# A new order of the operations of a fused attention and feed-forward kernel

## The chip, the cores and the metric

The kernel runs on one core of a Trainium2 chip. The core has engines that run their own instruction queues in order and wait for each other through semaphores: TensorE (PE, with the weight loads shown apart as PEld), VectorE (DVE), ScalarE (ACT), GpSimd (POOL) and SyncE (SP, which only issues DMAs here). The metric is the device time of one execution in microseconds. Before the change the median of three runs is 359.96 us (360.23, 359.96 and 359.49).

## The reference

Attention with a squared ReLU in place of a softmax, and a feed-forward layer with an exact GELU behind it:

```python
q, k, v: (8, 12, 448, 64)           # batches, heads, rows, head width
scores = q @ k^T / sqrt(64)
attn   = max(scores, 0) ** 2 / 448
x      = (attn @ v), heads side by side   # 3584 x 768
h      = x @ w_in                    # 768 x 2048
g      = 0.5 * h * (1 + erf(h / sqrt(2)))
out    = g @ w_out                   # 2048 x 768, float32
```

There is no sum over a row of scores, so the tiles of scores are independent of each other.

## The kernel before

**Loads and turning.** GpSimd loads Q, K, V and the weights with DMAs that cast float32 to bf16 (`nk`, `nq`, `v_sb`, `win_sb`, `wout_sb`). Scores need K and Q with the head width on the partitions (`kT`, `qT`). For batches 0 and 1 TensorE turns them (L620 and L648, tile `tp`) and VectorE or ScalarE copies the result out (L519, L521). For batches 2 to 7 SP issues DMA transposes (L675), one for K and one for Q of each head group; a head group is four heads, a batch has three. Some loads of later batches stand on GpSimd behind a small copy (L709, L717, tile `gate`) that waits until a Q transpose has landed, since the loads write over what the transposes read.

**Attention.** For each batch, head group and block of 128 keys (two heads of 64): scores (L752, `ps`), ReLU with scale into bf16 (L769 on ScalarE or L771 on VectorE, `a_sq`), the square (L781 on VectorE or L779 on ScalarE). When all seven blocks of a head group are done comes the product with V, called AV here (L831, `pav`), whose result is copied to `xT` (L519 or L521). In batches 0 and 1 some scores and AVs are done in halves of 224 rows.

**First product of the feed-forward layer.** A part of batch 0 is done plainly (L891, `psh`, GELU L901). Most of it is done in units by a scheme of seven products in place of eight (L1048, `pe`; sums of x `t_x` L1007, sums of weights `ws` L962), whose partial results VectorE and ScalarE add up (L1086, L519, L521, `part`) before GELU (L1098) writes `h_sb`. The last batch has its own form (L1199, L1236, L1245, L1164).

**Second product.** It goes by groups of 256 output rows (L1375, `pso`, with sums of hidden rows `s_sb` L1356 and sums of weights `t_sb` L1309). Passes add up the products into an output tile `osb` (L1409, L519 and L521); there are three output tiles. Each half of a group, 128 rows, is stored by SP when its passes are done (L1328, L1336). In the first batches a store of 128 rows is issued in two pieces, since attention rows lie in DRAM in four strides of 112.

**What sets the order.** Every step is an object `Op` with the engines that may do it, what it depends on and which buffers it takes and frees: three score tiles of two PSUM banks each (`w`), two more PSUM banks (`f`), 14 tiles `a_sq`, three output tiles. A string `ORDER` (lines 84 to 171, 1618 words) lists all of them. The letter of a word is the engine: P for TensorE, Q for TensorE with the two halves of a score tile in two separate banks of `f`, A ScalarE, D VectorE, G GpSimd, S the DMAs of SP. The number is the step, by the order in which the code creates it. Z is a product of zeros with so many columns (`fill`, L1677) that writes nothing that is used. `place()` walks through the string and puts each step at the end of its engine's queue, so the queue of each engine is the string's words of that engine in the string's order; nothing is decided at run time. Before the string's first words stand the loads of the first part of K and Q and nine products of zeros (`spin`, L1510).

Of the kernel before, what the change touches and what calls it, by code (L numbers as in the profile page):

```python
# [83 lines left out]
G0 G1616 G1 G3 G4 G7 D13 Z1024 A10 G118 A16 G2 P14 D15 P11 D12 P17 D18 P19 D20 P42 A43 P36 A37 P33  # L84
P21 D44 D22 P23 A24 D34 P51 P25 A52 D26 P48 Q39 D35 G117 P54 A49 D40 P63 A64 D55 P57 P27 D28 P29 D30
P69 P66 A58 D59 P31 D32 A70 D71 A67 G121 G6 G125 D38 P90 P93 D41 A94 D65 P131 A132 P102 A103 P129
P45 A46 A47 G126 Z672 A91 P84 D130 Q159 D50 D68 P72 G5 A160 D85 G8 G122 A73 G120 P111 A112 A53 D56
D74 P75 P133 D76 P156 D113 A157 A134 P81 D82 P139 A140 P60 D61 D83 P96 P108 D62 A97 D109 P137 P78
A79 D86 D80 P174 A175 D77 D92 P135 A136 D95 G124 P171 A172 D104 D98 P87 A88 P105 D89 A106 P168 A169
P141 A142 P162 D107 D110 D138 P195 A163 P99 D100 Q114 G119 P207 D101 D176 P165 A196 A115 D116 A158  # L90
P198 A199 D173 P143 A144 D208 D170 A166 D197 P240 A241 A161 D250 D251 P180 D181 D167 G128 G123 G9
D164 P222 A223 P192 P242 A243 P244 D253 D209 P145 A193 A146 P213 A214 A245 D194 P177 A178 D200 P189
A179 P183 D215 D190 D191 P246 A184 A247 P210 D182 A211 P216 P186 A187 D185 P248 A249 P258 P275 A217
D254 G127 G236 D188 P219 A276 G235 G238 G147 A220 Q201 D224 D212 D255 G148 P204 A202 A203 A205 D252
A221 P260 P277 A206 D259 P261 P278 A262 D409 D280 D218 D257 P265 D256 P282 A283 A266 Q225 A279 D412
D263 P270 P267 A226 A227 D371 D372 P284 D268 A269 P287 D285 P375 A264 A281 P392 A393 P273 G150 D271
P290 D288 P382 P399 D447 D374 A376 P378 P395 A274 D373 D450 A289 A291 D448 G151 P377 D451 P394 D397
A286 A400 A383 P387 P404 D380 A396 A379 P384 A272 D405 A406 P401 D388 P413 P430 A389 A414 A431 D385
A386 P420 P437 A421 D402 S228 A438 P407 D452 P390 D410 P416 A391 D411 P433 A408 D455 P442 S229 D454
A417 A434 P415 A398 G153 G154 P432 D443 A444 D435 A436 D418 P422 P439 A403 Q299 A300 P314 A315 P425  # L100
D423 P428 D456 D426 P459 A427 A424 D440 G234 A419 P311 P317 P445 P461 A441 D453 D449 D457 A318 D460
S230 S231 P463 P323 D312 A429 A381 A446 A313 D462 S232 P308 D316 S233 D301 A324 D309 D464 P350 P465
D466 A351 D352 P305 P302 A306 D310 P335 A307 P467 G237 G149 G152 G155 D458 D336 D468 A303 D304 P469
D470 P326 A327 P365 A366 P341 A342 D319 P471 P338 G239 G292 A339 A340 P320 D491 D472 A321 P332 A322
D337 D492 D343 G293 G294 D493 A333 P329 G295 D330 D367 S475 S476 P495 G296 A496 P497 P353 D498 P359
D334 D360 A331 A354 P362 A363 P499 S473 A500 P501 P356 P347 D325 A364 D328 P344 A357 A358 D355 D348
G297 D361 D345 D346 D349 G481 P511 A512 P520 A521 P503 P517 D502 A518 P526 P368 A369 D527 A519 P514
D504 S477 S478 G484 D494 S479 S480 P529 P505 D370 D583 P587 A513 P604 P507 D584 D515 G298 P594 A530
G487 A588 P589 A595 D605 D586 D522 A528 P607 P590 D508 D585 D592 P611 A516 P606 D608 A591 G482 G483
D621 D609 P599 A612 G485 G486 P596 S657 D531 P613 G488 D600 A601 S658 G489 S510 P623 P640 G663 D597  # L110
D614 P616 D617 A610 A641 A624 D622 P602 D506 P619 P625 P642 A593 A615 A603 A620 A598 Q523 D628 D645
A524 A646 P535 P626 P643 D525 S509 A536 A627 P630 P647 P538 A539 D631 D644 Q532 D533 A618 A534 P571
A572 P632 D648 P649 D673 P635 Q550 P553 A554 P652 D650 A651 D633 P638 P655 A656 D551 D674 A639 D636
A637 P677 P577 D653 A654 P559 A560 P547 S659 P679 D552 D675 P565 D548 S660 A678 D680 A578 A555 D540
P562 D563 D537 A566 S661 A567 D676 P681 P683 A682 D684 A634 P541 P574 P544 A545 D546 A629 A564 G666
P685 D686 S474 D542 D543 D693 D694 G490 P687 D688 S691 P689 D690 P568 A575 A549 A569 P556 D695 P719
A557 A558 A720 P713 D714 P697 D698 P725 A726 A727 A576 P728 D729 P722 D696 A570 P699 S692 D700 P731
P737 D732 P701 D702 D723 P703 P705 P746 D579 S662 G669 G664 G665 A561 D573 A747 P580 G667 A581 D704
D706 D730 D582 D785 P716 P709 A717 D710 S712 G668 G670 D786 P789 D788 G671 P806 A724 D790 P791 D794
D807 A738 P796 P813 D814 P707 A718 D787 A733 D715 P808 A739 D811 D708 A721 A812 P809 P792 D823 A810  # L120
P749 A750 Q734 D793 P740 A741 A795 D797 P798 P815 D816 P818 D819 D799 A742 A735 A736 D748 P825 P842
A843 P801 P821 P804 A751 A805 Q770 D802 P752 S711 A822 D826 P828 P845 A846 P832 D824 D753 D829 P849
D875 P827 S859 S860 S861 P844 D754 A850 P854 A800 S862 P834 P851 A771 A803 P879 D855 D830 D852 A833
D835 D847 P837 A817 A820 A853 P840 P857 P764 D876 D838 P755 D765 D877 A880 P883 A756 D878 A836 A858
A831 P773 A774 P761 D762 P881 D882 A841 G865 G868 A848 A884 P743 A763 A839 P767 D768 P918 D766 A775
P885 D886 P887 G672 D757 D888 A744 A856 A919 D745 P889 D890 D772 S893 P933 A934 D895 A935 P758 A759
D896 P779 A780 P776 A777 S863 A760 P891 P899 A900 S864 D898 P945 P927 D892 A778 P921 A922 A928 D946
D781 A947 P903 D920 P901 D897 P942 P948 A949 D769 D943 P782 A783 P924 G871 D902 A904 P930 D929 D931
D932 A925 P905 D906 A784 P907 D908 G866 P951 P915 D923 P939 D987 P909 G867 A940 D926 G869 G870 G872
D910 D988 P911 D912 S914 A952 P991 P1008 A916 A917 D990 Q963 D964 D944 P957 G873 A953 S1061 A958  # L130
D959 P936 A937 Q954 A938 P998 P1015 D992 P993 P1010 D1009 S1062 D989 A999 D950 P1011 A1016 A955
D1013 A1014 A956 P994 D996 P1003 D1012 A995 P1020 P1027 D1025 P1044 P1000 D1021 A1022 D1004 D1028
A1045 D1001 P1029 A997 P1046 D1049 A1050 D1032 A1005 P1030 P1047 D1026 P1017 D1018 A1031 P1034 P1051
D1048 S1063 S1064 S1065 A1002 P1023 P1036 P1053 D1052 D1054 A1035 D1037 P1039 P1056 P1006 G1067
A1007 G1070 D1057 D1079 A1024 P1042 P1059 A1060 P1081 D1040 S913 P978 A1041 A1043 A1058 P1117 D941
A979 P960 A961 D1077 D1078 D1118 P1150 D1151 S894 D962 P1120 P1083 A1121 P966 P972 A1082 P969 A973
P1085 P1141 D980 D967 D1084 A970 D1086 A968 D974 D1080 P981 A982 G874 A1055 P975 P1087 D1088 D1142
P1089 A1033 D1090 A976 P1091 A983 A1019 D1092 A1038 P1144 P1132 D1097 D977 P1147 A965 D971 A1133
A1148 D1134 P1093 P1101 D1094 S1095 S1066 P1129 A1130 P984 A1119 P1126 D1099 D1098 P1103 A985 A986
D1102 P1105 D1104 D1127 A1106 A1145 P1107 P1135 A1131 P1123 P1156 A1124 D1122 P1109 D1143 P1195  # L140
G1073 G1068 A1125 D1136 A1157 P1193 D1189 P1212 G1069 G1071 G1072 D1137 A1149 S1263 P1210 D1108
D1110 P1111 D1100 P1113 G1074 D1128 A1211 D1215 P1165 A1194 G1075 D1198 D1112 S1115 A1199 A1166
A1167 D1114 P1138 D1190 D1192 S1264 S1265 Q1153 S1096 P1200 P1217 P1196 P1213 A1139 A1154 D1140
A1218 Q1177 A1201 D1227 A1197 P1159 A1160 P1205 A1214 P1222 D1191 A1216 P1229 P1246 P1219 D1223
A1224 S1116 D1206 D1178 A1247 D1220 P1231 S1266 P1248 D1251 S1267 A1230 G1617 P1232 P1249 A1161
A1221 P1202 A1233 D1234 A1235 P1225 A1250 D1228 A1207 D1158 D1203 A1226 P1236 P1253 A1152 P1238
# [1568 lines left out]
```

## Time and profile before

| | |
|---|---|
| median of three runs | 359.96 us |
| the profiled execution | 360.24 us |
| its span | 358.5 us |
| TensorE busy | 350.0 us, 98% |
| VectorE busy | 305.6 us, 85% |
| ScalarE busy | 270.3 us, 75% |
| GpSimd busy | 102.9 us, 29% |
| mean granted clock of TensorE | 0.999 |

The span is the time from the first to the last recorded instruction or transfer; the execution takes 1.74 us more. A row of the timeline gives the start in us from the start of the span, the length, the engine, the line, the operation, the tiles (written <- read) and the shapes; in brackets stands how long the engine had been idle and what released it. SPq and POOLq rows are the issue of a DMA, not its transfer. A row of the DMA issues gives the time from issue to landing at its end. A row of the groups gives busy time, mean length in ns, idle time ahead and its releasers.

### The profile page before, as it was taken

The page shows a single profiled execution, that of the slowest core. Times are in us where ns is not written, and L with a number is a line of the kernel's source. Part 1 is how long each engine was busy: PE and PEld are TensorE (multiplying, and loading weights), DVE is VectorE, ACT ScalarE, POOL GpSimd, SP SyncE. Part 2 cuts the span into 40 slices and gives each one's busy share as a digit, 9 for nine tenths or more (in the row PEclk, how much of TensorE's full clock was granted, in tenths as well). Part 3 has the DMA queues.
Part 4 walks back from the last instruction along what each step waited for, and adds up shares of the span by engine and source line. Part 5 has one row for each costly group of instructions (what it writes and reads, how often), then busy time and mean ns, then how long its engine had stood idle before and what let it go on. Part 6 is the DMA issues. An engine that isn't in the chain of part 4 may idle for free.

```text
span 358.5 us, 9223 instructions
## 1 busy us (share of the span) xinstructions
PE 350.0 (98%) x3841; PEld 248.0 (69%) x3841; DVE 305.6 (85%) x515; ACT 270.3 (75%) x437; POOL 102.9 (29%) x138
## 2 busy tenths in 40 slices
PE   8879999999999999999999999999999999999995
PEld 3557679955588655896557965579668855788663
DVE  2999999999997989988889898779988998595762
ACT  3999997899869896978978669789986778334300
POOL 8664816096193104700075100841000000000000
PEclk9999999999999999999999999999999999999999
DMA  9999999999999958995399941998402001012222
GB/s 171 197 201 204 201 204 157 146 145 148 183 141 146 214 84 127 154 169 79 63 90 159 214 69 51 88 171 209 72 3 90 2 0 46 3 44 90 88 87 91
DMA packets 124361, 43.01 MB, mean 120 GB/s; under 512 B 102688, under 2 KB 120992, under 8 KB 124320
## 3 DMA queue, kind: packets, MB, share of 16 engines
q0 software_dynamic: 85328, 22.47, 66.2%
q1 hardware_dynamic: 38448, 19.50, 26.0%
q8 instruction: 30, 0.49, 0.5%
q10 hardware_dynamic: 544, 0.46, 0.4%
q14 instruction: 11, 0.09, 0.1%
HBM read 45.61 MB, written 11.01 MB: 158 GB/s over the span
## 4 chain that ended last, share of the span: by engine, by line
PE 92%; ACT 5%; DVE 2%; issue 0%; DVEq 0%; ACTq 0%
PE pso L1375 37%; PE pe L1048 30%; PE ps L752 9%; PE pav L831 8%; PE pb L1199 4%; ACT a_sq L769 3%; PE psh L891 2%; PE spin L1510 1%; DVE a_sq L781 1%; DVE a_sq L771 1%; ACT xT L521 0%; PE tp L620 0%; PE fill L1677 0%; ACT a_sq L779 0%; ACT qT L521 0%
## 5 line engine op out<-in xcount | busy, mean ns | idle before, releaser
L769 ACT ACTIVATE a_sq<-ps 128x896 bf16<-128x896 f32 (+1 forms) x125 | 106.7, 893 | 14.5 <-PE ps L752 14.2
L781 DVE TENSOR_TENSOR a_sq<-a_sq 128x896 bf16<-128x896 bf16 (+1 forms) x108 | 63.8, 615 | 2.1 <-ACT a_sq L769 1.9
L1375 PEld LDWEIGHTS <-s_sb 128*128 128x128 bf16 x456 | 42.4, 98 | 32.3 <-issue 7.1
L1048 PEld LDWEIGHTS <-win_sb 128*128 128x128 bf16 x624 | 59.5, 98 | 2.7 <-issue 1.5
L771 DVE TENSOR_SCALAR a_sq<-ps 128x896 bf16<-128x896 f32 (+1 forms) x57 | 55.5, 988 | 2.6 <-PE ps L752 2.2
L779 ACT ACTIVATE a_sq<-a_sq 128x896 bf16<-128x896 bf16 x61 | 57.2, 959 | 0.5
L752 PE MATMUL ps<-qT,kT 64*64 64x448 bf16 (+1 forms) x756 | 49.7, 337 | 2.7 <-ACT a_sq L769 1.3
L1098 ACT ACTIVATE h_sb<-part 128x448 bf16<-128x448 f32 x78 | 43.2, 580 | 9.9 <-DVE part L1086 9.7
L1086 DVE TENSOR_TENSOR part<-pe,part 128x448 f32<-128x448 f32 x78 | 45.5, 620 | 5.3 <-PE pe L1048 3.6
L1375 PEld LDWEIGHTS <-h_sb 128*128 128x128 bf16 x336 | 31.9, 98 | 22.9 <-issue 4.0
L1048 PEld LDWEIGHTS <-ws 128*128 128x128 bf16 x468 | 44.1, 98 | 3.5 <-issue 2.9
L1375 PE MATMUL pso<-wout_sb,s_sb 128*128 128x384 bf16 (+2 forms) x232 | 41.1, 321 | 0.0
L1375 PE MATMUL pso<-t_sb,s_sb 128*128 128x384 bf16 x224 | 41.1, 327 | 0.0
L1375 PE MATMUL pso<-wout_sb,h_sb 128*128 128x384 bf16 x224 | 41.1, 327 | 0.0
L559 POOL DMA_DIRECT2D nk<-in_k_dram x36 | 34.7, 968 | 9.6 <-DMA wout_sb<-in_moe_w_out_dram 8.1
L831 PE MATMUL pav<-a_sq,v_sb 64*64 64x448 bf16 (+1 forms) x756 | 36.5, 329 | 0.8 <-DVE a_sq L781 0.8
L752 PEld LDWEIGHTS <-kT 64*64 64x64 bf16 x756 | 19.6, 105 | 23.7 <-issue 17.7
L1048 PE MATMUL pe<-t_x,win_sb 128*128 128x224 bf16 x312 | 34.5, 259 | 0.0
L1048 PE MATMUL pe<-xT,win_sb 128*128 128x224 bf16 x312 | 34.1, 259 | 0.0
L1048 PE MATMUL pe<-t_x,ws 128*128 128x224 bf16 x312 | 33.2, 259 | 0.0
L521 ACT COPY part<-pe 128x448 f32<-128x448 f32 x53 | 26.4, 541 | 8.9 <-PE pe L1048 6.2
L1409 DVE TENSOR_TENSOR osb<-pso,p_sb 128x384 f32<-128x384 f32 x42 | 23.3, 554 | 9.4 <-PE pso L1375 5.9
(74 smaller groups left out, 409.5 us busy)
## 6 DMA issues: line engine op xcount, KB each, us to landing
out_dram<-osb SPq DMA_DIRECT2D x19, 384.0 KB, 2.8
nq<-in_q_dram POOLq DMA_DIRECT2D x38, 112.0 KB, 5.8
nk<-in_k_dram POOLq DMA_DIRECT2D x36, 112.0 KB, 5.8
v_sb<-in_v_dram POOLq DMA_DIRECT2D x5, 672.0 KB, 7.6
v_sb<-in_v_dram POOLq DMA_DIRECT2D x9, 224.0 KB, 8.0
win_sb<-in_moe_w_in_dram POOLq DMA_DIRECT2D x8, 192.0 KB, 9.2
wout_sb<-in_moe_w_out_dram POOLq DMA_DIRECT2D x4, 384.0 KB, 12.7
wout_sb<-in_moe_w_out_dram POOLq DMA_DIRECT2D x1, 1536.0 KB, 15.8
```

Source lines behind the costliest of these rows:

```text
L521: A.copy(dst, src)
L559: nc.gpsimd.dma_start(nk[b][:, g0, :, e], rows[:, e].rearrange("p (i d) -> p i d", d=D))
L752: nc.tensor.matmul(side(ps, e)[64 * j : 64 * j + 64, x * w : x * w + w], kT[r, g, i * 128 + 64 * j : i * 128 + 64 * j + 64], moving, start ...
L769: A.activation(to, x, AF.Relu, scale=c_att)
L771: V.tensor_scalar(to, x, c_att, 0.0, op0=mybir.AluOpType.mult, op1=mybir.AluOpType.max,)
L779: A.activation(ar, ar, AF.Square)
L781: V.tensor_mul(ar, ar, ar)
L831: nc.tensor.matmul(side(pav[0], e)[o2 : o2 + 64, :w], vt[b][r, 2 * g + e, bass.ts(i, D)], box["a2"][r, e, o : o + w], start=(i == 0), stop ...
L1048: nc.tensor.matmul(bank[name][:, y, z * HS : z * HS + HS], w[:, k, bass.ts(mm, 128)], right()[:, k], start=first and k == 0 and z == 0, st ...
L1086: V.tensor_add(get(to), ps(name), get(other))
L1098: A.activation(h_ring()[:, m : m + 2, o + half[c].start : o + half[c].stop], src().rearrange("p (x n) -> p x n", x=2), AF.Gelu,)
L1375: nc.tensor.matmul(box[bank][:, n0:n1], left()[:, kf], right()[:, kf, n0:n1], start=bool(need) and kf == 0, stop=kf == K2 - 1, skip_group_ ...
```

## The change

The string `ORDER` is replaced; nothing else changes. The same 1618 steps are listed. 101 steps move from ScalarE to VectorE and 91 the other way: among them, ScalarE has 121 of the full-width ReLUs where it had 116, 59 of the squares where it had 61, 21 of the AV copies where it had 33. The queue of GpSimd is unchanged. On TensorE most steps shift by a few places; six score or AV steps change between the two kinds of banks. On SP some stores and transposes change places. The lines with the beginning and with the first stores:

```diff
@@ -84,88 +84,88 @@
-G0 G1616 G1 G3 G4 G7 D13 Z1024 A10 G118 A16 G2 P14 D15 P11 D12 P17 D18 P19 D20 P42 A43 P36 A37 P33
+G0 G1616 G1 G3 G4 G7 D13 Z1024 A10 G118 A16 Z672 P14 D15 G2 P11 D12 P17 P33 D34 G117 A18 P36 A37 P21
...
-D337 D492 D343 G293 G294 D493 A333 P329 G295 D330 D367 S475 S476 P495 G296 A496 P497 P353 D498 P359
+P356 P499 A357 G297 D333 D325 A334 D355 P501 P347 A364 S474 D358 A348 S473 S475 S476 A500 P359 D360
...
```

On TensorE at the start of the program (`fill` are the products of zeros, `tp` the first turning of K), before:

```order
L1510 MATMUL spin_106<-zero_100 128x512
L1677 LDWEIGHTS zero_100
L1677 MATMUL fill_130<-zero_100 64x512
L1677 LDWEIGHTS zero_100
L1677 MATMUL fill_130<-zero_100 64x512
L620 LDWEIGHTS nk_119
L620 MATMUL tp_140<-ident_95,nk_119 64x128
```

and after:

```order
L1677 MATMUL fill_130<-zero_100 64x512
L1677 LDWEIGHTS zero_100
L1677 MATMUL fill_139<-zero_100 64x512
L1677 LDWEIGHTS zero_100
L1677 MATMUL fill_139<-zero_100 64x160
L620 LDWEIGHTS nk_119
L620 MATMUL tp_142<-ident_95,nk_119 64x128
```

The second product of zeros, of 672 columns, has moved from the 28th place among TensorE's steps to the one behind the first.

On SP near 85 us, before: the transposes of batch 2's last head group (`kT_1483`, `qT_1482`), those of batch 3's first (`kT_1856`, `qT_1855`), and the store of rows 128 to 255 in two pieces. The store of rows 0 to 127 stands 14 places further behind.

```order
L675 DMA_TRANSPOSE kT_1483<-nk_1148 128x7x128
L675 DMA_TRANSPOSE qT_1482<-nq_1147 128x8x112
L675 DMA_TRANSPOSE kT_1856<-nk_1148 128x7x128
L675 DMA_TRANSPOSE qT_1855<-nq_1147 128x8x112
L1336 DMA out_0_dram<-osb_1697 96x768
L1336 DMA out_0_dram<-osb_1697 32x768
```

and after, with batch 2 as `kT_1212` and `qT_1211`, batch 3 as `kT_1936` and `qT_1935`, and both stores:

```order
L675 DMA_TRANSPOSE kT_1212<-nk_904 128x7x128
L675 DMA_TRANSPOSE qT_1211<-nq_903 128x8x112
L1336 DMA out_0_dram<-osb_1683 112x768
L1336 DMA out_0_dram<-osb_1683 16x768
L1336 DMA out_0_dram<-osb_1742 96x768
L1336 DMA out_0_dram<-osb_1742 32x768
L675 DMA_TRANSPOSE kT_1936<-nk_904 128x7x128
L675 DMA_TRANSPOSE qT_1935<-nq_903 128x8x112
```

Four store pieces now stand ahead of the first K and Q transposes of batch 3. The first of them waits for the last pass of rows 0 to 127. On VectorE, before, that pass is the third row from the end here:

```order
L1409 TENSOR_TENSOR osb<-pso,osb 128x384
L781 TENSOR_TENSOR a_sq<-a_sq 128x896
L1409 TENSOR_TENSOR osb<-pso,p_sb 128x384
L781 TENSOR_TENSOR a_sq<-a_sq 128x896
L1356 TENSOR_TENSOR s_sb<-h_sb 128x1024
L1409 TENSOR_TENSOR osb<-pso,osb 128x384
L781 TENSOR_TENSOR a_sq<-a_sq 128x896
L1356 TENSOR_TENSOR s_sb<-s_sb,h_sb 128x1024
```

and after it is the last row:

```order
L1409 TENSOR_TENSOR osb<-pso,osb 128x384
L781 TENSOR_TENSOR a_sq<-a_sq 128x896 x2
L1409 TENSOR_TENSOR osb<-pso,p_sb 128x384
L1356 TENSOR_TENSOR s_sb<-h_sb 128x1024
L1356 TENSOR_TENSOR s_sb<-s_sb,h_sb 128x1024
L1356 TENSOR_TENSOR s_sb<-h_sb 128x1024
L1409 TENSOR_TENSOR osb<-pso,osb 128x384
```

The pass has moved behind all three sums of hidden rows.

More of the change, by code (lines that the diff above doesn't have):

```diff
@@ L89 @@
[L89 to L103, printed above, removed]
@@ L109 @@
[L109 to L123, printed above, removed]
@@ L124 @@
[L124 to L134, printed above, removed]
@@ new lines @@
+D134 D82 D140 A80 A112 D98 P156 P135 D92 P141 D83 D136 P168 G128 A157 G123 G9 A77 G127 G236 D104
+P174 A142 A169 P87 D113 D88 D89 D110 Q171 A172 P162 P99 A163 D175 D176 G235 G238 Q114 A100 A101 P195
+D161 P213 G147 A115 G148 G150 G151 G153 D164 A116 D252 P165 A166 A196 D214 D167 P143 A144 P240 P192
+P180 A241 A193 P222 D197 A223 A181 P244 A245 P242 D158 P198 A199 D173 D250 P207 A243 D170 D182 D208
+P177 A178 P189 A179 D190 D191 P183 A184 P145 A146 P204 A185 D251 P186 P210 P248 A187 A205 D200 D254
@@ new lines @@
+P246 D255 D188 A249 A247 A211 P258 P275 P219 A220 D194 D209 A259 D253 D224 Q201 A276 P216 A217 A218
+D257 P260 S228 S229 D215 P261 P278 D202 A279 P277 P265 P282 A262 D256 G154 P267 P284 D263 A206 A283
+P287 A264 D221 D212 A203 D409 Q225 A226 A227 D285 S230 A286 D266 P270 D280 G234 D268 P273 A274 D288
+D371 P375 P392 A393 A281 A376 P290 D271 D372 D374 P382 P399 A269 A291 P395 A383 A400 P378 P377 P394
+P387 A396 A379 A289 D447 D373 P384 D412 P401 D410 D397 A398 D380 P413 D388 A389 P404 D385 P430 A386
@@ new lines @@
+P905 A784 D906 D929 A947 P939 A940 P915 P942 D943 A926 P907 D908 P909 D941 D987 D988 D910 P911 D912
+A916 D917 P991 A920 P1008 D990 Q963 D964 P957 A923 P936 Q954 A958 A953 P998 P1015 A950 A1016 D989
+D937 D938 P993 D992 P1010 D1009 D1013 D996 P994 D955 P1011 A999 P1003 A995 P1020 G869 A1012 G870
+G872 D1021 A1022 D1004 P1027 P1044 S914 D1025 P1000 D1001 P1029 P1046 D1026 A997 A1028 D1032 S1061
+A1045 D1049 A959 G873 P1030 P1017 A1014 P1047 D1048 P1006 A1002 P1034 A1033 P1051 A944 A1005 D1031
+P1036 P1053 D1018 P1023 D1035 D965 A1052 P1056 D1037 S1062 D1054 P1039 A1024 S893 D1077 A1055 A1007
@@ new lines @@
+P1042 A1043 Q1117 S913 A1118 D956 P960 D1040 D1057 P966 A1041 D967 D1078 A1038 A961 A962 P1059 A1060
+P1081 P1120 A1082 S1063 S1064 D968 A1121 P978 D1079 P972 D979 D980 A973 D974 P1083 P975 A976 P1123
+P969 A970 A1050 P1085 D1124 P1135 A1019 P1141 P981 A1058 A1142 D1084 D1086 P1087 A1119 D982 A983
+D1080 P1089 G1067 D1088 A1136 P1091 D977 P1132 P1147 A1148 D971 D1097 P984 D1090 G1070 D1133 A1134
+P1150 G874 D1151 A985 D986 D1092 S1095 P1144 A1145 P1093 D1094 D1143 P1126 A1127 A1128 S1065 D1098
@@ new lines @@
+P1156 P1129 A1130 D1100 D1131 P1101 P1195 P1212 S1066 G1073 G1068 D1102 G1069 D1125 P1193 P1210
+D1099 A1211 D1215 A1216 P1103 D1104 P1105 P1107 D1194 D1198 A1157 D1106 D1108 P1109 D1110 D1191
+P1111 D1112 D1189 P1113 D1114 D1190 A1137 P1165 A1158 A1122 P1138 D1139 A1199 A1166 Q1153 A1154
+P1200 P1217 D1192 A1146 A1201 D1140 P1196 D1155 P1213 D1227 G1071 P1159 G1072 A1218 A1214 Q1177
+S1263 A1160 P1222 A1178 D1197 P1205 D1206 P1229 P1246 A1247 D1223 A1224 P1219 D1220 P1231 P1248
+D1179 A1230 A1149 D1234 P1202 D1203 P1232 A1207 P1249 A1235 G1074 A1221 A1233 D1251 A1252 D1250
@@ new lines @@
+S1116 S1264 P1208 A1209 D1228 P1236 G1075 P1253 S1265 S1266 P1238 A1237 D1239 G1617 A1254 D1167
+P1225 P1241 D1242 A1204 P1255 D1256 A1226 A1240 A1161 P1171 Q1168 D1169 A1243 A1172 S1096 P1258
+D1152 D1259 P1244 P1261 A1257 Q1174 P1162 A1262 A1245 S1267 A1260 D1175 A1176 D1269 D1270 P1183
+A1184 D1185 P1301 A1302 P1273 D1271 D1274 P1275 P1307 D1272 A1308 P1180 D1276 A1163 P1277 A1181
+A1170 D1164 P1279 D1278 P1281 P1298 A1299 P1289 D1173 D1182 P1186 D1280 D1282 D1290 A1309 P1295
+D1187 A1296 P1292 G1076 D1188 D1361 D1363 A1293 P1285 D1286 S1288 S1268 D1362 P1367 S1115 D1291
@@ new lines @@
+P1365 P1382 A1383 D1364 D1294 P1372 P1283 A1366 D1370 D1373 P1368 A1369 D1284 A1371 P1384 D1387
+P1389 A1300 D1390 P1385 A1386 D1399 P1304 A1305 A1306 Q1313 D1475 P1377 P1394 D1378 A1388 P1401
+P1418 D1395 D1400 D1402 A1314 A1379 P1374 P1391 P1403 P1420 D1392 P1397 A1398 D1419 D1423 A1424
+D1406 A1393 A1407 P1404 P1421 P1408 P1425 D1375 P1380 D1422 D1297 A1405 D1409 P1410 D1426 A1381
+A1303 P1427 P1430 P1413 D1411 A1376 P1340 A1341 D1435 Q1310 D1431 D1414 A1415 D1428 A1311 A1312
+P1328 A1329 P1355 D1342 P1416 P1433 A1417 P1439 A1434 D1476 A1432 D1436 D1356 P1352 A1429 D1438
@@ new lines @@
+A1440 P1346 D1347 D1437 A1396 A1348 P1337 P1441 D1338 A1353 A1354 P1443 P1325 D1442 A1444 A1339
+D1357 P1322 P1331 D1315 A1323 D1332 A1324 P1445 D1446 P1447 P1349 P1343 D1333 P1449 D1448 P1451
+A1350 P1316 D1344 D1345 A1412 S1287 D1455 A1351 P1358 A1326 A1327 P1319 D1452 D1450 D1457 A1320
+D1456 P1459 P1461 D1359 A1460 P1463 D1360 A1317 D1330 A1321 D1318 D1462 D1464 P1334 A1335 S1453
+A1336 D1477 D1479 D1478 P1465 D1458 P1481 P1498 D1466 A1482 P1467 P1485 D1549 P1483 P1500 D1550
+D1484 D1468 P1469 P1487 P1471 D1470 A1499 D1501 P1504 D1472 D1488 P1489 P1502 D1505 S1474 P1506
@@ new lines @@
+D1507 D1480 P1555 D1490 A1491 P1509 P1553 D1554 P1492 D1493 P1512 A1503 A1486 P1515 P1532 D1510
+P1517 P1534 D1513 A1508 D1552 A1533 P1536 P1495 A1516 D1551 D1535 P1538 S1473 D1496 A1497 D1518
+S1454 P1557 D1556 D1558 P1523 P1540 P1519 D1539 D1541 A1542 P1521 D1522 A1511 D1524 A1494 P1559
+A1514 A1520 P1543 D1544 P1546 D1560 P1529 P1526 D1547 D1527 P1561 D1562 D1530 A1548 P1563 D1564
+A1525 A1537 A1528 A1545 P1565 A1531 P1573 D1569 D1570 D1566 S1568 S1567 D1571 P1575 D1574 P1577
+D1576 P1579 D1572 D1578 P1581 D1580 D1591 D1582 P1583 D1589 D1590 D1584 S1587 P1585 D1586 S1588
@@ L172 @@
+P1593 D1594 P1595 D1596 P1597 D1598 S1609 P1599 D1600 D1592 P1601 D1602 S1610 P1603 D1604 S1611
+P1606 P1605 D1607 S1612 D1608 S1613
 """
```

78 lines of the change are left out of this document (33 added, 45 removed).

## The prediction

> **What bounds the kernel now.** I read the page first (busy shares, slices, chain), then the busy time by stretches, and then the timeline and the DMA issues at the places where the order differs. On the page:
>
> ```profile
> span 358.5 us, 9223 instructions
> PE 350.0 (98%) x3841; PEld 248.0 (69%) x3841; DVE 305.6 (85%) x515; ACT 270.3 (75%) x437; POOL 102.9 (29%) x138
> PE 92%; ACT 5%; DVE 2%; issue 0%; DVEq 0%; ACTq 0%
> ```
>
> TensorE is busy 98% of the span and holds 92% of the chain that ended last. The change keeps every operation, so it can save only what TensorE waits, and that is little; it can cost whatever makes TensorE wait where it now does not. Three stretches show where the waits are:
>
> ```profile
> 8.00:32.00 24.00, 20.46 (x530) 14.26 (x522) 23.66 (x45) 23.96 (x36) 14.86 (x22) 1.00 1.33 198
> 32.00:44.00 12.00, 12.00 (x145) 8.61 (x139) 11.40 (x20) 11.25 (x18) 8.63 (x11) 1.00 1.31 202
> 44.00:70.00 26.00, 26.00 (x303) 23.87 (x300) 25.54 (x40) 22.29 (x44) 7.89 (x10) 1.00 1.72 175
> ```
>
> The columns are window, length, and busy time of PE, PEld, DVE, ACT and POOL. From 8 to 32 us TensorE has 24.00 - 20.46 = 3.54 us idle, while VectorE (23.66) and ScalarE (23.96) have almost none: there the evictions are the bound. From 32 us on TensorE has no idle at all. The largest group of it, in the first stretch:
>
> ```profile
> L752 PE MATMUL ps<-qT,kT 64*64 64x224 bf16 x164 | 7.5, 263 | 2.1 <-ACT a_sq L769 0.8 <-DVE a_sq L771 0.6 <-DVE qT L519 0.3
> ```
>
> 2.1 of the 3.54 us is scores that wait until a relu has emptied a bank.
>
> **The change, part 1: the head.** These rows are the places in the first 30 us that the new order touches:
>
> ```profile
> 4.94 1.06 PE L1677 MATMUL fill<-zero 64*64 64x512 bf16 x2
> 5.93 0.44 PE L620 MATMUL tp<-ident,nk 128*64 128x128 bf16 x8
> 8.04 1.35 ACT L769 ACTIVATE a_sq<-ps 128x448 bf16<-128x448 f32 x2 [2.27 <-PE ps L752]
> ...
> 16.72 0.44 PE L1677 MATMUL fill<-zero 64*64 64x512 bf16 x2
> ...
> 26.48 0.86 PE L831 MATMUL pav<-a_sq,v_sb 64*64 64x224 bf16 x28 [0.79 <-DVE a_sq L781]
> ```
>
> The second fill (672 columns) runs at 16.72 now, in a stretch in which TensorE idles anyway, so it costs nothing there. The new order puts it right behind the first fill, ahead of the first turning of K (5.93). That turning starts when the first fill ends, and ScalarE then waits 2.27 us for the first scores: nothing covers work put in there. Its price is 0.44 us by its own row, or 0.99 x 672/1024 = 0.65 us by the first fill, which takes 5.93 - 4.94 = 0.99 us for 1024 columns at that time. I take 0.65, the row nearest in time. Since the evictions have no idle time up to 32 us, a later start is passed on in full.
>
> Against it stands the AV at 26.48, which waits 0.79 us for a square on VectorE. In the new order the two score operations that it needs stand 13 places earlier on TensorE and the AV itself two places later, so this wait goes: -0.79. The sum of the head is +0.65 - 0.79 = -0.14 us. Its ends: nothing is won and the fill costs 0.65; or more waits than that one go. How much can go is limited by two rows. VectorE and ScalarE do the same evictions ahead of 44 us in both orders and have 0.60 and 0.75 us idle between 32 and 44 us, so about 0.7 us is what a better sharing leaves. And the first score of batch 2 needs a transpose that lands at 60.42 + 8.0 = 68.4:
>
> ```profile
> 60.42 1.25 SPq L675 DMA_TRANSPOSE qT<-nq  x1
> qT<-nq SPq DMA_TRANSPOSE x1, 8.0
> ...
> 69.90 0.57 PE L752 MATMUL ps<-qT,kT 64*64 64x448 bf16 x8
> ```
>
> It starts at 69.90, so at most 1.5 us won earlier would arrive anywhere. With 1.4 us won and the fill at 0.44, the lower end of the head is -0.96.
>
> **Part 2: the steady stretch.** 101 evictions, squares and passes move from ScalarE to VectorE and 91 the other way; most places on TensorE shift by a few operations. In a stretch where TensorE does not wait, this is worth nothing, and it costs something only where a product gets closer to what it reads. The closest such place is near 54 us: the first product of the next unit of batch 0 stood four products behind the last AV of batch 1, and now stands two behind.
>
> ```profile
> 52.56 1.31 PE L1048 MATMUL pe<-t_x,win_sb 128*128 128x224 bf16 x12
> 94.65 1.15 DVE L519 CAST xT<-pav 128x448 bf16<-128x448 f32 x2
> ```
>
> Two products (12 matmuls) last 1.31 us; the two copies of an AV last 1.15 us. That still covers, so I take 0; if an engine comes to it late, one copy (some 0.6) is the price.
>
> The other place is the output tiles, three in all. A pass can take one only when the store that read it has landed. The new order leaves the second half of group 1 unstored until some 170 us (it stands beside operations that run then now), so that two tiles serve from 125 to 170 us, and the first pass of the next group takes one whose store was issued just before it:
>
> ```profile
> 133.22 1.76 SPq L1336 DMA_DIRECT2D out_dram<-osb  x4
> 137.23 0.55 DVE L1409 TENSOR_TENSOR osb<-pso,p_sb 128x384 f32<-128x384 f32 x1
> out_dram<-osb SPq DMA_DIRECT2D x1, 288.0 KB, 2.7
> ```
>
> That store is issued at some 133.2 and lands 2.7 us later at 135.9, and the pass runs at 137.23 now: 1.3 us of cover, so 0, and at most one us if the pass comes earlier.
>
> **Part 3: the stores ahead of the transposes.** This is the term that decides. On SP's queue the K and Q transposes of batch 3, first head group, stand at 81.98 and 83.84 now, ahead of the store at 85.16. In the new order both stores of the first output group (rows 0 to 127 and 128 to 255, four pieces) stand ahead of these two transposes.
>
> ```profile
> 81.98 1.63 SPq L675 DMA_TRANSPOSE kT<-nk  x1
> 83.24 0.56 DVE L1409 TENSOR_TENSOR osb<-pso,p_sb 128x384 f32<-128x384 f32 x1
> 83.84 1.23 SPq L675 DMA_TRANSPOSE qT<-nq  x1
> 84.24 0.69 DVE L1356 TENSOR_TENSOR s_sb<-h_sb 128x1024 bf16<-128x1024 bf16 x1
> 84.84 0.56 DVE L1409 TENSOR_TENSOR osb<-pso,osb 128x384 f32<-128x384 f32 x1
> 85.16 1.61 SPq L1336 DMA_DIRECT2D out_dram<-osb  x2
> 86.87 1.47 SPq L675 DMA_TRANSPOSE kT<-nk  x1
> ...
> 92.50 2.10 SPq L675 DMA_TRANSPOSE kT<-nk  x1
> 94.22 0.55 PE L752 MATMUL ps<-qT,kT 64*64 64x448 bf16 x8
> 95.00 1.72 SPq L675 DMA_TRANSPOSE qT<-nq  x1
> ...
> 110.83 2.41 SPq L1336 DMA_DIRECT2D out_dram<-osb  x4
> ```
>
> The first of these stores waits for the pass at 84.84. In the new order this pass stands on VectorE behind the pass of 83.24 and three sums of hidden rows (84.24 to 84.84 is 0.60 each), so it ends at about 83.24 + 0.56 + 3 x 0.60 + 0.56 = 86.2. SP's queue is in order: nothing behind a store that waits is issued. Four pieces then take 2.41 us by the row at 110.83, so the K transpose is issued at about 88.6 instead of 81.98, and the Q transpose 1.86 us behind it (81.98 to 83.84), at about 90.5. How long they take to land is read from the issues, each in its own window:
>
> ```profile
> kT<-nk SPq DMA_TRANSPOSE x1, 6.9
> qT<-nq SPq DMA_TRANSPOSE x1, 7.8
> nq<-in_q_dram POOLq DMA_DIRECT2D x2, 112.0 KB, 8.9
> kT<-nk SPq DMA_TRANSPOSE x1, 8.3
> kT<-nk SPq DMA_TRANSPOSE x1, 5.5
> qT<-nq SPq DMA_TRANSPOSE x1, 3.7
> ```
>
> They are the issues at 81.98, 83.84, 85.44 (the last two loads of batch 3), 86.87, 92.50 and 95.00. Now the pair has landed at 88.9 and 91.6, and the first score of batch 3 reads it at 94.22: 2.6 us of cover. The pair will start some 6.6 us later, so the cover is gone; only shorter landings can give some back. With the 5.5 us of the issue at 92.50 the Q transpose lands at 96.0, and TensorE waits 96.0 - 94.2 = 1.8 us. A second reading counts the traffic: by 95.2 (86.87 + 8.3) all loads, this pair, one store and one further transpose have landed now; in the new order the same, with a second store in that transpose's place, is what has to be through: 95.2, a wait of 1.0. I take 1.4 between the two. The ends: 3.7 us, as for the issue at 95.00, after the last load landed (85.44 + 8.9 = 94.3): 94.2, no wait. And the trace has one sequence of the same kind, four pieces of a store and behind them the pair of the next group, with the last loads issued just before:
>
> ```profile
> 115.16 3.53 SPq L675 DMA_TRANSPOSE qT<-nq  x1
> qT<-nq SPq DMA_TRANSPOSE x1, 7.3
> ```
>
> With 7.3 us the transpose lands at 97.8 and the wait is 3.6. I take less, because another pair stood in the queue ahead of those stores. The Trainium skill, DMA: Bandwidth & Descriptors, section "Queues, rings and completion order", says that each DMA engine takes the descriptors of one ring in ring order, so the transposes would get through behind the four pieces whatever else is in flight; by it the sum would be the one with 7.3 us, 363.4.
>
> What waits behind the score is everything on TensorE, since its order is fixed, and from 32 us to the end it has no idle time that could take this up. Behind the pair on SP stand the other transposes of batch 3, at 86.87 and after, and GpSimd's gate copy, which holds back the loads of batch 4, waits for the same Q transpose. The first reader of all these is the next head group of batch 3:
>
> ```profile
> 111.37 0.57 PE L752 MATMUL ps<-qT,kT 64*64 64x448 bf16 x8
> ```
>
> A delay of some 5 us stays far below what lies between. I cost both at nothing. The last products, passes and stores of the kernel stand as before.
>
> **The sum.** The profiled execution took 360.24 us, of which 358.5 are span and 1.74 lie around it; it stands 0.28 above the median of 359.96. 360.24 - 0.14 (head) + 1.4 (wait at 94 us) = 361.50, less 0.28: **361.2 us**.
>
> **Rivals.**
>
> *The wait is as long as in the twin sequence.* The Q transpose takes 7.3 us: 3.6 us of wait, 360.24 - 0.14 + 3.6 - 0.28 = 363.4. For it speaks that loads, stores and the pair follow each other in the same way; against it, the pair that is missing ahead.
>
> *The pair is hidden anyway.* It lands within 3.7 us, at 94.2: 360.24 - 0.14 - 0.28 = 359.8, no measurable change. The loads would have to be through by 90, some 4 us earlier than now; for this speaks that no transposes run beside them between 82 and 88. Also against the forecast: if my count of VectorE's work is late by a microsecond, half the wait goes. The Trainium skill, same page and section, says that a DMA engine takes turns between the queues that it has work for; by it, loads that share with nobody for 6 us are through earlier, and the time would be this 359.8. The trace agrees as far as 8.3 us with loads beside it and 3.7 without.
>
> *Faster: the head gives its waits back.* Place: scores and AV between 8 and 32 us; 1.4 of the 3.54 us of idle go, the fill costs 0.44, and the pair is in time: 360.24 - 0.96 - 0.28 = 359.0. It decides when more than 1.2 us of that idle goes and the Q transpose takes under 4 us. Against it stands that ScalarE and VectorE are busy 99% there.
>
> **How the numbers follow.** 0.2% (0.72 us) is about what a measurement of this kernel can tell from no change. Chances: short wait 361.2, 0.40; long wait 363.4, 0.20; hidden 359.8, 0.22; faster 359.0, 0.18. Slower by over 0.72 means above 360.68: all of the long wait and 0.34 of the short one (below 0.9 us of wait it is no measurable change), 0.54. Same: 0.22 + 0.06 = 0.28. Faster 0.18. The range goes from 358.9 (just below the faster case) to 363.6 (just above the long one) and leaves out about 0.1 on each side; the likeliest case alone spans 360.7 to 362.2, with waits of 0.9 to 2.4.
>
> **What would show it.** In the profile after: TensorE idle before a score of L752 at some 94 us, with a transpose of Q as releaser; on SP two stores, then K and Q transposes issued at about 88.6 and 90.5; the second fill at 6 us, the first turning of K 0.4 to 0.65 later; no wait at the AV near 26 us. The forecast is wrong if the pair lands before 94 us, if the stores are issued before 85 us, or if TensorE's idle between 8 and 32 us changes by more than a microsecond.

## The result, and the profile after

The new order takes 362.27 us in the median of 17 runs, the kernel before 360.14 us in 17 runs beside them. The ratio is 1.0057, with a 95% interval of 1.0039 to 1.0075: slower by 2.1 us. The runs of the new order scatter from 359.53 to 364.39 us, those of before from 359.49 to 360.89. Runs of before stand beside every experiment too; one of the 35 beside e1 to e4, at 593.73 us and a mean clock of 0.559, is a slow one and is left out of the ratios. The profiled execution took 363.33 us, 3.09 more than that of before.

The page after: the span, the busy time by engine, and the granted clock of TensorE in 40 slices.

```profile
span 361.6 us, 9216 instructions
PE 350.8 (97%) x3841; PEld 248.4 (69%) x3841; DVE 310.0 (86%) x523; ACT 265.0 (73%) x428; POOL 103.0 (29%) x138
PEclk9999999999899999999999999999999999999999
```

TensorE has the same work. New is one slice of the clock at eight tenths, the eleventh, which begins at 90.4 us. The busy time by stretches, with the columns as before (PEclk is the third number from the right):

```profile
8.00:32.00 24.00, 20.78 (x524) 15.19 (x519) 23.66 (x44) 23.78 (x40) 14.89 (x22) 1.00 1.34 199
44.00:70.00 26.00, 26.00 (x305) 24.18 (x294) 24.84 (x41) 22.05 (x45) 7.63 (x10) 1.00 1.81 178
90.00:110.00 20.00, 17.69 (x185) 11.79 (x184) 14.55 (x26) 12.04 (x18) 10.44 (x14) 0.91 1.48 158
```

In the head TensorE idles 3.22 us where it idled 3.54. From 90 to 110 us it now idles 2.31 us, and its clock is 0.91. The timeline there, with the passes of group 0 on VectorE, SP's queue, and TensorE:

```profile
82.00 0.56 DVE L1409 TENSOR_TENSOR osb<-pso,p_sb 128x384 f32<-128x384 f32 x1
84.40 0.55 DVE L1409 TENSOR_TENSOR osb<-pso,osb 128x384 f32<-128x384 f32 x1
84.98 2.96 SPq L1336 DMA_DIRECT2D out_dram<-osb  x4
88.11 1.82 SPq L675 DMA_TRANSPOSE kT<-nk  x1
90.04 1.81 SPq L675 DMA_TRANSPOSE qT<-nq  x1
...
95.52 0.57 PE L752 MATMUL ps<-qT,kT 64*64 64x448 bf16 x8 [2.31 <-DMA qT<-nq]
96.02 2.61 PE L1375 MATMUL pso<-t_sb,s_sb 128*128 128x384 bf16 x8
98.56 0.96 PE L752 MATMUL ps<-qT,kT 64*64 64x448 bf16 x8
...
100.78 0.54 PE L752 MATMUL ps<-qT,kT 64*64 64x448 bf16 x8
```

The four store pieces go first, the pair of transposes behind them, and TensorE stands 2.31 us before the scores of batch 3, released by the Q transpose. The product behind takes 2.61 us for eight matmuls instead of the 1.48 us before:

```profile
94.70 1.48 PE L1375 MATMUL pso<-t_sb,s_sb 128*128 128x384 bf16 x8
```

The stretches of that place, after, show why:

```profile
96.00:98.00 2.00, 2.00 (x11) 1.01 (x8) 0.00 (x0) 1.67 (x2) 0.21 (x2) 0.55 0.96 181
98.00:99.00 1.00, 1.00 (x10) 0.25 (x12) 0.00 (x0) 0.00 (x0) 0.81 (x1) 0.50 0.89 168
99.00:100.00 1.00, 1.00 (x20) 0.52 (x16) 0.80 (x1) 0.37 (x1) 0.00 (x0) 0.70 0.86 79
100.00:101.00 1.00, 1.00 (x30) 0.56 (x20) 0.76 (x2) 0.55 (x1) 0.22 (x2) 1.00 0.77 82
```

TensorE's clock is halved 0.7 us behind the end of the wait, for 3.4 us: 0.55 on average from 96 to 98 puts the start at 96.2, and 0.70 from 99 to 100 the end at 99.6. The Trainium skill, TensorE: Matmul & The Clock Gate, section "Part 1: The HAM clock gate", tells of such a halving after an idle window of some 3.4 us; here a wait of 2.31 us was enough.

So the 3.09 us of this execution are: TensorE arrives at the scores at 95.52 - 2.31 = 93.21 instead of 94.22, -1.01; the wait, +2.31; and the half clock, +1.65 (from the first scores to those at 100.78 it takes 5.26 us, and 3.61 in e1 below, without the clock drop). That is 2.95. The remaining 0.14 lies behind that place, where TensorE idles 0.25 of the 236 us from 104 to 340 and before 0.00. Of the 1.01, 0.57 is there at the first turning of K already (5.36 against 5.93), and 0.32 is the idle time saved between 8 and 32 us.

This trace is of one of six runs with a mean clock of 0.995, at 363.1 to 364.4 us. The other eleven, the median run among them, have 0.998 or more and no trace. Five of these stand close together, at 362.24 to 362.43.

### The profile page after: what moved, and what is told of

Its sections match the earlier page's. It is cut to its first block, busy times and chain, and to the rows that moved or that the text cites. A ratio compares the mean times of both kernels' runs of the same rounds, so it can differ in the third digit from the quotient of the medians.

```text
span 361.6 us, 9216 instructions
## 1 busy us (share of the span) xinstructions
PE 350.8 (97%) x3841; PEld 248.4 (69%) x3841; DVE 310.0 (86%) x523; ACT 265.0 (73%) x428; POOL 103.0 (29%) x138
## 5 line engine op out<-in xcount | busy, mean ns | idle before, releaser
L769 ACT ACTIVATE a_sq<-ps 128x896 bf16<-128x896 f32 (+1 forms) x131 | 109.9, 889 | 19.4 <-PE ps L752 19.1
L781 DVE TENSOR_TENSOR a_sq<-a_sq 128x896 bf16<-128x896 bf16 (+1 forms) x110 | 64.7, 614 | 1.8 <-ACT a_sq L769 1.5
L771 DVE TENSOR_SCALAR a_sq<-ps 128x896 bf16<-128x896 f32 (+1 forms) x50 | 50.2, 1012 | 8.3 <-PE ps L752 8.3
L779 ACT ACTIVATE a_sq<-a_sq 128x896 bf16<-128x896 bf16 x59 | 55.8, 961 | 1.2 <-DVE a_sq L771 0.8
L1375 PE MATMUL pso<-t_sb,s_sb 128*128 128x384 bf16 x224 | 42.2, 333 | 0.0
L521 ACT COPY part<-pe 128x448 f32<-128x448 f32 x55 | 27.6, 537 | 15.2 <-PE pe L1048 11.6
L1048 PE MATMUL pe<-t_x,win_sb 128*128 128x224 bf16 x312 | 35.5, 259 | 0.0
L709 POOL COPY gate<-qT 128x16 bf16<-128x16 bf16 x10 | 3.4, 342 | 103.5 <-DMA qT<-nq 103.5
```

The lines of the kernel that those rows point to most:

```text
L521: A.copy(dst, src)
L769: A.activation(to, x, AF.Relu, scale=c_att)
L771: V.tensor_scalar(to, x, c_att, 0.0, op0=mybir.AluOpType.mult, op1=mybir.AluOpType.max,)
L779: A.activation(ar, ar, AF.Square)
L781: V.tensor_mul(ar, ar, ar)
L1048: nc.tensor.matmul(bank[name][:, y, z * HS : z * HS + HS], w[:, k, bass.ts(mm, 128)], right()[:, k], start=first and k == 0 and z == 0, st ...
```

## The experiments

**e1: the pair first.** The new order with the two transposes ahead of the two stores again.

```diff
-P501 P347 A364 S474 D358 A348 S473 S475 S476 A500
+P501 P347 A364 S475 S476 S474 D358 A348 S473 A500
```

> The new order with one edit: the K and Q transposes of batch 3's first head group stand ahead of the two stores of group 0 again. Theory A (the stores ahead of the pair make TensorE wait at 95 us, and the half clock behind that wait costs as much again): no wait at the first scores of batch 3, clock 1.00 in every stretch, and what the new order won in the head stays, so 358.9 to 359.6 and no run above 360.5. Rival B (the loss is in the other moved operations, output tiles or evictions): the time stays within 1 us of the new order's 362.27.

Measured: 359.82 us (12 runs, 359.49 to 360.06 but for two at 362.43), against 360.16 us of before on the same chip; ratio 0.9987 (0.9965 to 1.0008). The timeline of e1:

```profile
80.87 2.00 SPq L675 DMA_TRANSPOSE kT<-nk  x1
83.04 1.25 SPq L675 DMA_TRANSPOSE qT<-nq  x1
85.42 1.87 SPq L1336 DMA_DIRECT2D out_dram<-osb  x4
...
93.48 0.55 PE L752 MATMUL ps<-qT,kT 64*64 64x448 bf16 x8
...
97.09 0.55 PE L752 MATMUL ps<-qT,kT 64*64 64x448 bf16 x8
```

The places of four words of 1618 carry the whole loss: 2.45 us. TensorE arrives at 93.48 and does not wait. Theory A holds, though the median is 0.2 above its range; what else was moved costs nothing that the interval can tell. The two runs at 362.43 break its bound of 360.5. They have a mean clock of 1.00 and no trace; their cause is open.

**e2: the stores first, in the order of before.** The two words are taken out of their places further behind.

```diff
-D330 D367 S475 S476 P495
+D330 D367 S474 S473 S475 S476 P495
```

> The order of before with one edit: both stores of group 0 stand ahead of the pair of transposes. Theory A: the pair lands at about 95.5, TensorE arrives at 94.2 and waits 1.3 us, so 361.4; in executions in which the wait is long the clock drops too and the time is above 362.5, so the runs scatter by 2 us or more. Rival B: 360.1, as before.

Measured: 360.97 us against 360.16, ratio 1.0003 (0.9984 to 1.0022). Six of the 12 runs lie at 359.7 to 360.5 and six at 361.5 to 361.6; but the runs of before beside them have the same second group, nine of 35 there (e9). The trace is of the lower group, so a wait in the upper one is not ruled out. In the trace the expected wait is missing:

```profile
85.45 3.44 SPq L1336 DMA_DIRECT2D out_dram<-osb  x4
89.06 1.23 SPq L675 DMA_TRANSPOSE kT<-nk  x1
90.46 1.22 SPq L675 DMA_TRANSPOSE qT<-nq  x1
...
94.24 0.55 PE L752 MATMUL ps<-qT,kT 64*64 64x448 bf16 x8
```

The pair is issued even later than in the new order, and yet TensorE does not wait. The DMA issues of both kernels say what differs: of the new order the last two loads of batch 3 (issued at 84.24 and 85.07) and the Q transpose,

```profile
nq<-in_q_dram POOLq DMA_DIRECT2D x2, 112.0 KB, 6.7
qT<-nq SPq DMA_TRANSPOSE x1, 5.3
```

and of e2 the same (loads at 83.84 and 84.67):

```profile
nq<-in_q_dram POOLq DMA_DIRECT2D x2, 112.0 KB, 5.6
qT<-nq SPq DMA_TRANSPOSE x1, 3.4
```

In e2 the transpose lands at 90.46 + 3.4 = 93.9, 0.4 before TensorE arrives; in the new order at 95.3, 2.1 after it. Two things come together: the loads of batch 3 are through later in the new order, and TensorE arrives a microsecond earlier. My expectation took the landing of the new order's trace for granted and was wrong.

What the landing goes with is seen when e2 is put beside the other traces with four pieces ahead of the pair (us from the start of the span; the landings are issue plus time to landing):

| | first store issued | last load of batch 3 issued | it lands | Q transpose issued | takes | lands |
|---|---|---|---|---|---|---|
| new order | 84.98 | 85.07 | 92.4 | 90.04 | 5.3 | 95.3 |
| e3 | 85.50 | 85.60 | 92.6 | 90.38 | 5.3 | 95.7 |
| e7 | 85.61 | 85.71 | 93.1 | 90.75 | 5.4 | 96.2 |
| e2 | 85.45 | 84.67 | 91.1 | 90.46 | 3.4 | 93.9 |
| e8 | 85.72 | 84.56 | 89.3 | 89.40 | 3.7 | 93.1 |

Where GpSimd issues the last load just behind the first store, the Q transpose takes 5.3 to 5.4 us; where it does so 0.8 us or more ahead of it, 3.4 to 3.7. If this is the cause, a shift of a microsecond between GpSimd and SP makes or removes most of the wait; it is not shown, since no run moves the loads alone.

**e3: zeros in the wait.** The new order with products that nobody reads, in the score tile that the waiting scores then write over. This adds work that the computation does not need.

```diff
+                if blocks[0][:3] == (3, 0, 3):
+                    for _ in range(12):
+                        nc.tensor.matmul(
+                            side(ps, 0)[:D, :NB], ident[:D, :D], wout_sb[:D, 0, :NB],
+                            start=True, stop=True,
+                        )
```

> The new order, with 12 products of 512 columns put right in front of the scores that wait for the pair, into the same score tile, which those scores then write over; they take some 2.6 us in which TensorE would idle. Theory A1 (idle time makes the clock drop): clock 1.00 from 90 to 110 us in every run, no time above 362.6, median 361.3 (the wait stays, the 1.7 us behind it go). Rival A2 (the drop has another cause, such as what the transposes and loads do at that time): clock 0.5 from 96 to 99 us as in the new order and 362.3 or more.

Measured: 362.36 us, ratio 1.0053 (1.0037 to 1.0069); no run of 12 with a mean clock below 0.998, where the new order has six of 17 at 0.995. In the trace of e3 the transpose lands late too, at 95.7, and the clock stays:

```profile
94.00:98.00 4.00, 4.00 (x27) 1.93 (x25) 1.68 (x4) 1.44 (x2) 0.41 (x3) 1.00 0.85 173
98.00:102.00 4.00, 4.00 (x58) 2.56 (x58) 3.54 (x6) 2.93 (x4) 2.05 (x4) 1.00 0.94 131
...
93.56 2.53 PE L748 MATMUL ps<-wout_sb,ident 64*64 64x512 bf16 x11
95.75 0.38 PE L758 MATMUL ps<-qT,kT 64*64 64x448 bf16 x3
```

A1 holds against A2: with the same stores, loads and transposes, but TensorE busy, the clock does not drop. The median that I expected was too low, by my own arithmetic: the zeros always cost their 2.5 us, so 359.82 (e1) + 2.5 = 362.3, which is what was measured. The short runs are gone. The bound of 362.6 did not hold: 362.93, 362.99 and 363.80 came at a mean clock of 0.999 to 1.00, so these are no clock drop, and what they are is open.

**e4: the fill at the start, in the order of before.** `Z672` moves from behind `G126` to behind `A16`.

> The order of before with one edit: the fill of 672 columns stands behind the first fill instead of at 16.7 us. The prediction: its 0.44 to 0.65 us are passed on in full, 360.6 to 360.8. Rival (it runs before the first operands are there, or speeds up what follows): within 0.2 us of 360.1, or faster.

Measured: 360.55 us against 360.16, ratio 1.0008 (0.9989 to 1.0028): seven runs at 359.5 to 360.6 and five at 361.8 to 362.0, these at a full mean clock. The lower group is that of before, so in it the fill costs nothing that can be seen. What sets the upper group of e4 is open, since its trace is one of the lower; a cost of the fill in some executions is not ruled out.

**e6: the pair first, and the fill back at its old place**, the same question in the new order.

> The new order with the pair ahead of the stores, and the fill of 672 columns back at its old place at 16.7 us. Prediction's term for the fill: 0.44 to 0.65 us less than the 359.82 of the new order with the pair first, 359.2 to 359.4. Rival (the fill at the start costs nothing, or keeps the clock up): 359.8 or more.

Measured: 359.87 us, ratio 0.998 (0.9963 to 0.9996) against 360.16; e1 has 359.82. By the medians the fill costs nothing here either. The timelines of the first products are those of a second trace of before (e9, the second fill not there), e6 (not there), and e7 (there):

```profile
5.09 0.41 PE L620 MATMUL tp<-ident,nk 128*64 128x128 bf16 x8
```

```profile
5.53 0.41 PE L620 MATMUL tp<-ident,nk 128*64 128x128 bf16 x8
```

```profile
4.68 0.91 PE L1677 MATMUL fill<-zero 64*64 64x512 bf16 x4
5.85 0.41 PE L620 MATMUL tp<-ident,nk 128*64 128x128 bf16 x8 [0.26 <-DVE nk L519]
```

The start of the first turning varies from one execution to the next of the same kernel (5.93 in the first trace of before, 5.09 here), by more than the fill takes: the nine products of zeros ahead last 4.02 us in the one and 3.62 in the other, the first fill 1.06 and 0.62. With the second fill TensorE still has to wait 0.26 us for its operand in e7.

**e5: one store ahead of the pair.** The new order with rows 128 to 255 ahead of the pair and rows 0 to 127, which wait for the late pass, behind it.

```diff
-A364 S474 D358 A348 S473 S475 S476 A500
+A364 D358 A348 S473 S475 S476 S474 A500
```

> The new order with one of the two stores (rows 128 to 255, two pieces, which does not wait for the late pass) ahead of the pair of transposes and the other behind it. Theory A (TensorE waits because the pair is issued late and behind four pieces): the Q transpose is issued at some 86 us instead of 90 and lands by 93.5, the wait is 0 to 0.5 us, no clock drop, 359.8 to 360.4. Rival (any store ahead of the pair is enough, its transfer holds the ring up): a wait of 1 us or more, 361 or more.

Measured: 360.10 us (359.31 to 360.80) against 360.16, ratio 0.9989 (0.9973 to 1.0006). The Q transpose is issued at 85.61 and lands 6.3 us later, at 91.9; TensorE arrives at 93.20 and does not wait. So a store ahead of the pair does no harm in itself. The harm comes with the store that waits for the late pass: it holds back the issue of the Q transpose from 85.61 to 90.04.

**e7: a product ahead of the waiting scores.**

```diff
-D349 P520 A521 D345 D346 P511 A512 P503 D361
+D349 P503 P520 A521 D345 D346 P511 A512 D361
```

> The new order with the stores ahead of the pair as it has them, and on TensorE one product of group 1 (1.3 us) moved ahead of the two scores that wait for the pair. Theory A (the wait is landing minus arrival, and the clock drops only behind a wait of some 2 us): the wait falls from 2.3 to about 1.0, no clock drop, median 360.8 to 361.2, no run above 361.8. Rival (the clock drops whatever the length of the wait): runs with mean clock 0.995 as often as in the new order, up to 363.

Measured: 361.57 us (360.73 to 363.74), ratio 1.0040 (1.0020 to 1.0060); no run at 0.995, the lowest is 0.998. Of its trace, which is of a run of 362.39:

```profile
93.80 1.46 PE L1375 MATMUL pso<-t_sb,s_sb 128*128 128x384 bf16 x8
96.30 0.76 PE L752 MATMUL ps<-qT,kT 64*64 64x448 bf16 x12 [1.04 <-DMA qT<-nq]
97.69 0.38 PE L752 MATMUL ps<-qT,kT 64*64 64x448 bf16 x4 [0.64 <-ACT a_sq L769]
98.50 0.76 PE L831 MATMUL pav<-a_sq,v_sb 64*64 64x448 bf16 x12 [0.42 <-ACT a_sq L769]
```

The wait is 1.04 as expected, and the clock does not drop. But the product has left its place behind the scores, where it gave ScalarE time for the ReLUs: 0.64 + 0.42 us of new waits. The median is better than the new order by 0.7 us and not by 1.2; five runs break the bound of 361.8, up to 363.74, and have only this one trace. The three waits add up to 2.10 us of idle time between 95.26 and 98.50, nearly as much as the 2.31 of the new order, and the clock stays.

**e8: six zeros.** As e3 with 6 in place of 12.

> The new order with 6 instead of 12 products of 512 columns in front of the scores that wait (1.3 us, so about 1 us of idle time stays). Theory A1 (a shorter idle time does not make the clock drop): no run with mean clock 0.995, median 361.5 to 362.2, none above 362.8: the wait is the longer of the zeros and the landing. Rival (any idle time there does it): a group of runs at 0.995 and 363 to 364.

Measured: 362.17 us (360.92 to 363.79), ratio 1.0050 (1.0028 to 1.0072); no run at 0.995. In its trace the pair landed at 93.1, before the zeros began at 93.78, so a wait of one microsecond behind them was not seen and the question is not answered there. Three runs at 363.7 to 363.8 have a full mean clock, so time above the expected bound is there that is no clock drop; it has no trace and is open.

**e9: the second group of before.** The kernel before, unchanged, is traced twice more, since beside e1 to e4 nine of its 35 runs and beside e5 to e8 ten of 35 lie at 361.5 to 362.2, all with a mean clock of 0.995. None of the 17 beside the result does.

> The kernel before, unchanged, for a trace of its second group of times (about 361.6 at a mean clock of 0.995, some two runs in seven beside experiments e1 to e8). Theory H: the clock drops in the head, where TensorE idles; then such a trace shows half clock before 32 us. Rival P: the pair of transposes lands late there too; then half clock behind 94 us. A trace of the first group (about 360.0) shows neither and leaves it open.

> The same as the first look: theory H, half clock before 32 us; rival P, half clock behind 94 us; neither if the time is about 360.0.

The first execution took 361.66 us, the second 359.37. Stretches and timeline of the first:

```profile
24.00:28.00 4.00, 2.91 (x68) 2.20 (x72) 4.00 (x7) 3.98 (x6) 1.87 (x3) 0.89 1.24 205
28.00:32.00 4.00, 4.00 (x68) 2.83 (x63) 2.77 (x6) 3.12 (x5) 1.97 (x4) 0.68 1.25 204
...
26.69 1.16 PE L831 MATMUL pav<-a_sq,v_sb 64*64 64x224 bf16 x28 [0.79 <-DVE a_sq L781]
...
28.53 2.27 PE L891 MATMUL psh<-xT,win_sb 128*128 128x224 bf16 x12
```

stretches of the second:

```profile
24.00:28.00 4.00, 3.09 (x69) 2.29 (x70) 4.00 (x9) 4.00 (x7) 1.92 (x3) 1.00 1.23 202
28.00:32.00 4.00, 3.93 (x90) 2.83 (x88) 3.90 (x10) 4.00 (x7) 2.12 (x3) 1.00 1.21 199
```

and the first of these stretches in the trace that the prediction reads:

```profile
24.00:28.00 4.00, 2.75 (x72) 1.72 (x64) 4.00 (x8) 4.00 (x7) 2.11 (x4) 1.00 1.24 205
```

Theory H holds for this execution: the clock is halved for 3.4 us again, from 27.1 to 30.5, behind the AV that waits 0.79 us, in a stretch in which TensorE is idle a quarter of the time. Twelve plain products take 2.27 us there and 1.32 in the trace of before that the prediction reads. But the same wait of 0.79 or 0.80 us stands in the other two traces of before, at a full clock. Just ahead of the drop, from 23.70 to 27.11, TensorE is busy 2.11 of 3.41 us; at the same work in the trace that the prediction reads, from 23.50 to 26.90, it is busy 2.10 of 3.40. So these gaps are where the drop happens, and they do not decide by themselves whether it does. The new order has closed this gap: TensorE is busy 3.75 us from 24 to 28, and the AV does not wait. None of the 72 runs of e1, e3, e5, e6, e7 and e8, which share its head but for the fill in e6, has a mean clock of 0.995. The clock drop in the new order's trace is at another place, 96.2 us.

## Why the prediction was right

The direction, and the place that decides, were right: e1 takes the loss away with one edit there. The size was too small: 1.2 us were forecast (359.96 to 361.2) and 2.1 measured (360.14 to 362.27). The 362.27 lies just above the 360.7 to 362.2 of the likeliest case. That it still lies well inside the range is in part luck, since the upper end was kept open for the long wait, 363.4, which did not happen in that way. Point by point:

- *The stores ahead of the pair.* Right, and e1 shows that it is the whole loss. The issue of the pair was forecast at 88.6 and 90.5 and is 88.11 and 90.04. The first store was forecast at 86.2 and is 84.98, just ahead of the 85 that I named as a sign of being wrong: VectorE came to the pass that was at 83.24 by 82.00 already, and the three sums behind it took 1.84 us, as counted. The pieces took 2.96 us instead of 2.41; the Q transpose landed 5.3 us after its issue, near the 5.5 that I took.
- *The wait* was mis-sized: 1.4 forecast, 2.31 in the trace. The landing was right (1.4 behind 94.2 is 95.6; it is 95.3); the arrival was not. I set the landing against the arrival of before, 94.22, and TensorE arrived at 93.21. My own sum for the head would have moved it by 0.14 only; the rest is mostly a start of the program that was 0.57 earlier in this execution, and that varies from one execution to the next.
- *What the wait costs* is the step that failed: the wait of 1.4 was counted once, and nothing was set down for the clock behind it. The half clock cost 1.65 us more in the profiled execution. The mean clock says that six of 17 runs have it; they are the runs at 363.1 to 364.4, which no case of mine held but the long wait, by another cause. In e3, with the idle time filled, no run has it. It is not what sets the median: the median run has a mean clock of 1.00. Taking 1.65 off those six runs gives an estimate of 361.7 for the median, so some 0.6 us of the 1.1 above the forecast. The five runs at 362.24 to 362.43 fit the 359.82 of e1 with a wait of some 2.5 us, but none of them has a trace, and e1 (two runs at 362.43) and e4 (five at 361.8 to 362.0) have long runs at a full clock that the wait does not explain.
- *The head.* The wait of 0.79 us at the AV is gone, as forecast. The fill at 0.65 us was wrong: the first turning of K, forecast 0.4 to 0.65 later, is 0.57 earlier in the trace, e1 with the fill is 0.05 shorter than e6 without, and e4 shows no cost in its lower group. What I took as its place, a queue where nothing covers it, holds a wait for the first operand (0.26 in e7) and an uncertain start. With the pair first the new order is at 0.9987 of before (0.9965 to 1.0008), so a gain of the head is not shown by these times; e6, at 0.998 (0.9963 to 0.9996), is clear of no change by little. What the head does win is the clock (e9): no drop in 72 runs, against 19 of 70 of before.
- *The steady stretch and the output tiles* at nothing: right to 0.25 us. TensorE is busy 26.00 of 26.00 us from 44 to 70 and 235.75 of 236 from 104 to 340, in e1 as well. A pass on VectorE does wait 0.31 us for a store's landing, at 140.06, where I saw 1.3 us of cover; TensorE does not feel it.
- *The rival that the pair is hidden* is seen in single traces of other orders: in e2 and e8 the loads are through by 91.1 and 89.3 and the pair has landed at 93.9 and 93.1. With no transposes issued between 82 and 88, the loads were faster, as the rival has it: 4.7 to 7.4 us for the last one in these five traces, against 9.5 before (85.44 to 94.9; the 8.9 of my row is the middle of two loads). Whether the short runs of the new order, from 359.53 us on, are of this kind is not shown, since none has a trace.
- *Ring order* (the Trainium skill, DMA: Bandwidth & Descriptors, section "Queues, rings and completion order", cited for the long wait): the trace agrees as far as the transposes land behind the stores (the last piece by 94.0, the pair at 94.6 and 95.3). But the Q transpose took 5.3 us and not 7.3, and the profiled execution came to its 363.33 by a shorter wait and the half clock.

## What to carry to other kernels

When one queue issues both stores and the transfers that the bounding engine is about to need, put a store that waits for late work behind those transfers: here the Q transpose was issued at 90.04 instead of 83.04 (e1). The wait is landing minus arrival, with the arrival of the new order and not of the old. Ask also what a wait does to the clock: a wait of 2.31 us cost 1.65 us more, and one of 1.04 us (e7) cost no clock. And read an order for the places whose cover is below the scatter of a landing: the same Q transpose behind the same four pieces took 3.4 to 5.4 us.

## What was not expected of the hardware

The halved clock lasts 3.4 us in both traces that have it, and it comes after far less idle time than that. In the new order one wait of 2.31 us stands ahead of it. In 19 of 70 runs of before, by the one trace of these, it comes after gaps of at most 0.79 us: TensorE was busy 2.11 of the 3.41 us ahead of the drop. Neither the longest gap nor the sum of the gaps decides it alone. The profiled execution of before kept the full clock with the same gaps in the same place (busy 2.10 of 3.40 us), and e7 kept it with 2.10 us of idle time in 3.24, in three waits of at most 1.04. What does decide is open. And the start of the program shifts by up to 0.8 us between executions of one kernel (5.93 and 5.09 for the first turning).
